# Epsilon as a column, balancing sums in PSUM, a lag of two blocks: eight small edits to a TensorE-bound kernel of attention and mixture of experts

## The chip, the cores and the metric

One core of a Trainium2 chip. The metric is device time in microseconds (us), the median of several runs; less is better. The engines are TensorE (PE in the profile, PEld its weight loads), VectorE (DVE), ScalarE (ACT), GpSimd (POOL) and SyncE (SP), whose queue issues the DMAs.

## The reference

Banded attention followed by a mixture of experts whose gate matrix is balanced by alternating row and column sums.

```python
# attention: q, k, v are (4, 8, 768, 64); n_global = 8, n_local = 96
scores = scale * q @ k.T + bias(|i - j|, head)       # kept where j < n_global or 0 <= i-j < n_local
a = np.exp(scores - max); a = a / (a.sum(-1) + 1e-09)
x = (a @ v) laid out as (3072, 512)
# experts: w_gate (512, 8), w1 (8, 512, 1024), w2 (8, 1024, 512)
P = np.exp(x @ w_gate - max)
for _ in range(8):
    P /= P.sum(1, keepdims=True) + 1e-09
    P /= P.sum(0, keepdims=True) + 1e-09
    P *= N / E
out = sum over e of P[:, e:e+1] * (np.maximum(x @ w1[e], 0) @ w2[e])
```

## The kernel before

All arithmetic is float32 precise: every operand is split into a high and a low part, and each product is three matmuls (high x low, low x high, high x high). The 3072 tokens are 24 tiles of 128, in three batches of 8 tiles (`BT`); the hidden columns are 31 groups (`NG`) of 256, the first 256 of expert 0 being done beside the attention. Within a batch, layer 1 of a group is a fast matrix product in seven products instead of eight (`FIRST`: p1 to p7, in banks x, y, z, w). The operands t1 to t4 that it needs are sums of blocks of x, made by `right_sums` on POOL or, for the last half batch, by `part_sum` on VectorE.

There are three stages in time.

1. *Attention*, to about 270 us. 32 units (4 batches, two halves, 4 pairs of heads) of three groups each. `softmax` (masked maximum on VectorE, line 342) and `exponentials` (ScalarE, line 356, which accumulates the row sums `sm`), then `inverses`: epsilon added (367), reciprocal (368), copied out to a tile (370) that `invert` turns on TensorE. Work of expert 0 (`filler`: h_ps, fhop, y_ps), the gate, and the block sums (lines 749 to 754) run between; `LEADS` says at which point of the last unit parts of the block sums of the last half batch are issued.
2. *The last batch, plainly*, about 270 to 930 us. For each group `layer1_fast`, then for each of 8 tiles a second layer (`layer2`, into y_ps), which is multiplied by the gate weight and added to `acc` (line 1235; for expert 0, line 1231, unweighted, and line 1234 multiplies by the weight of expert 0 once). Layer 1 of a group is interleaved with the second layer of the group before by `together(one, two, each, lead)`: one step of each in turn; with a `lead` of n, the second begins n steps later and what is left of it is handed back. The balancing (`sinkhorn`, 8 iterations of eight small VectorE operations and one matmul) runs through the first groups in steps, and its result `pm` is first needed by the second layer of the first group of expert 1, which runs beside layer 1 of the fifth group. Meanwhile ScalarE and POOL prepare the weights of later groups (`make_group`, lines 635, 636, 653).
3. *The other two batches, fast*, from about 930 us. Both layers use the seven products. `Fast.ended` makes the operands of the second layer (VectorE line 936, ScalarE 924, POOL 925 and 930). The second layer's seven products (m_ps, two PSUM buffers of two banks) are added up over 30 groups in SBUF tiles `ms` (line 1391; 1389 for the first group). After the 30th group `COMBINE` adds the seven sums together on POOL (line 1393). The 31st group is plain again: its y blocks are weighted and added to `acc`, and `back` turns the combined blocks on TensorE (c_ps) and adds them to `acc` (1411); then the tile goes out by DMA (1210). y_ps and c_ps share the two buffers of m_ps, except in the last batch, where y_ps uses the four banks of layer 1. `acc` is reloaded from DRAM with the part done in stage 1, and multiplied by the gate weight of expert 0 (line 1371), in group 2 of each batch.

The order on TensorE is that of the program (line 100 and 103 are the helper that keeps it). On the other engines a planner sets it: the framework simulates the program with its own costs and places each instruction when its inputs are ready. `issue_after` holds instructions behind a named one. PSUM tiles wait for the release of the buffer that they reuse.

The order of the products of the last combining group and of the tiles, which decide what must be ready first:

```python
LAST = tuple(SECOND[n] for n in (0, 3, 4, 2, 1, 6, 5))   # p1, p7, p6, p5, p3, p4, p2
ORDER = [n for i in (1, 0) for n in range(i, BT, 2)]     # 1, 3, 5, 7, 0, 2, 4, 6
BLOCKS = (("p2", "p4"), ("p3", "p5"))                    # turned for even and for odd tiles
```

Of the kernel before, what the change touches and what calls it, by code (L numbers as in the profile page):

```python
# [8 lines left out]
F32 = mybir.dt.float32  # L9
# [8 lines left out]
P = 128  # L18
# [25 lines left out]
LAST = tuple(SECOND[n] for n in (0, 3, 4, 2, 1, 6, 5))  # L44
COMBINE = {"p1": (("p6", "p1"),), "p6": (("p5", "p6"),), "p5": (("p3", "p5"), ("p5", "p7")),
           "p4": (("p4", "p6"), ("p4", "p7")), "p2": (("p2", "p1"),)}
# [59 lines left out]
class Banded:  # L106
# [4 lines left out]
    RAW = 4 * UT * P  # L111
    LEADS = (6 * CHUNK, 8 * CHUNK)

# [209 lines left out]
    def softmax(self, t, s_list):  # L323
# [37 lines left out]

    def inverses(self):

        nc, D = self.nc, self.D
        for n in self.summed:
            sm = self.sums[n]
            nc.vector.tensor_scalar(out=sm, in0=sm, scalar1=EPS, scalar2=None, op0=ALU.add)
            nc.vector.reciprocal(out=sm, in_=sm)
# [226 lines left out]
class Moe:  # L595
# [168 lines left out]

    def relu_split(self, src, t):
        nc = self.nc
        nc.scalar.activation(out=t[:, 0], in_=src, func=AF.Relu)
        self.low = nc.vector.scalar_tensor_tensor(out=t[:, 1], in0=src, scalar=0.0, in1=t[:, 0], op0=ALU.max,
                                                  op1=ALU.subtract)
# [96 lines left out]
    def sinkhorn(self, ps, tag):  # L866
# [16 lines left out]
        for _ in range(SINKHORN_ITERS):  # L883
            rsum = small.tile([P, TT], F32, name="rsum")
            nc.vector.tensor_reduce(out=rsum, in_=pm, op=ALU.add, axis=AX.X)
# [7 lines left out]
            nc.vector.tensor_reduce(out=csum, in_=c_ps.rearrange("p t e -> p e t"), op=ALU.add, axis=AX.X)  # L893
            nc.vector.tensor_scalar(out=csum, in0=csum, scalar1=EPS, scalar2=float(E) / N, op0=ALU.add, op1=ALU.mult)
# [55 lines left out]
def pipeline(tc, attention, ident, moe, acc):  # L950
# [11 lines left out]
    with ExitStack() as top:  # L962
# [126 lines left out]
        first, second = slice(0, 1), slice(1, KH)  # L1089
        stages = list(zip(attention.LEADS, ((("t1", slice(0, KH)),), (("t3", first), ("t2", first), ("t4", first)))))  # L1090
        tail = [(("t3", second),), (("t2", second), ("t4", second))]
# [119 lines left out]

        def plain_ops():
            hs = {}

            def ended(name, bank):
                hs[name] = hop.tile([P, 2, BU], F32R, name="hop")
                moe.relu_split(bank, hs[name])
            return hs, ended
# [3 lines left out]
        def second_plain(b, g, w, hs, new_ps, last, scaled, between=None):  # L1222

            e = groups[g][0]
            first_scaled = scaled is False and e != 0 and groups[g - 1][0] == 0
            for k, n in enumerate(ORDER):
                y_ps = new_ps(k)
                moe.layer2(n, w, hs, y_ps)
# [3 lines left out]
                else:  # L1232
                    if first_scaled:
                        nc.scalar.mul(a, a, moe.pm[:, tt, 0:1])
                    nc.vector.scalar_tensor_tensor(out=a, in0=y_ps, scalar=moe.pm[:, tt, e:e + 1], in1=a,  # L1235
                                                   op0=ALU.mult, op1=ALU.add)
# [32 lines left out]
        for g in range(NG):  # L1269
# [6 lines left out]
            def each(n):  # L1276
# [8 lines left out]
            prev = second_plain(b, g, w2, hs, lambda k: yps.tile([P, DM], F32, name="y_ps", tag="y"),  # L1285
                                g == NG - 1, False)
        for _ in sinkhorn:
            pass
# [38 lines left out]
        moe.in_order = False  # L1327
        mp = None
        for q, b in enumerate(order):
            x_ops, x_next = x_next, {}  # L1330
            ms = {}
            for g in range(NG):
# [7 lines left out]
                else:  # L1340
                    hs, ended = plain_ops()

# [19 lines left out]
                two = pend.pop(0)  # L1362
                rest = together(moe.layer1_fast(x_ops, w, mps, ltmp, ended), two, each, 0 if g < PLAIN else 2)
                if q == 0 and g == 0:
                    pss.close()
                    mp = top.enter_context(tc.tile_pool(name="mp", bufs=2, space=PSUM, reuse_waits="tile"))
                if g == 2:
                    for n in range(2):
                        nc.sync.dma_start(out=acc[:, n * HB:(n + 1) * HB], in_=y_spill[2 * b + n])
                    for n in range(BT):  # L1370
                        nc.scalar.mul(acc[:, n], acc[:, n], moe.pm[:, b * BT + n, 0:1])
                for load in loads:
# [3 lines left out]
                if g < PLAIN:  # L1376
                    def second_fast(hs=hs, w2=w2, g=g, ms=ms, seq=seq):
                        for p, a, o in seq:
# [11 lines left out]
                            else:  # L1390
                                nc.vector.tensor_tensor(out=ms[p], in0=bank, in1=ms[p], op=ALU.add)  # L1391
                            for to, by in COMBINE.get(p, ()) if g == PLAIN - 1 else ():
                                nc.gpsimd.tensor_tensor(out=ms[to], in0=ms[to], in1=ms[by], op=ALU.add)
                            yield
                    pend.append(second_fast())
                else:
                    last = q + 1 == len(order)

                    def new_ps(k, last=last):
                        if last:  # L1400
                            return mps.tile([P, BU], F32, name="y_ps", tag="h")
                        return mp.tile([P, 2, BU], F32, name="y_ps", tag="m")[:, 0]

                    def back(k, n, ms=ms):
# [85 lines left out]
```

## Time and profile before

| | us |
|---|---|
| median of 3 runs (lowest, highest) | 2115.78 (2114.74, 2116.29) |
| the profiled execution | 2115.21 |
| its span | 2113.4 |
| TensorE busy | 2089.2 |
| POOL busy | 1501.5 |
| VectorE busy | 1491.9 |
| ScalarE busy | 741.3 |

The granted clock of TensorE is 0.999 over the span. "Busy" of TensorE counts a matmul from its start to its modelled end, so that consecutive matmuls overlap; waits are read from the lists of who waited for whom and from the timeline, where the figure in brackets is the idle time of the engine before that instruction and the instruction that ended it. In a timeline row the columns are start, duration, engine, line, operation, output<-inputs, sizes, count. In a row for one line of the code the three numbers are the least, median and greatest duration in ns.

### The profile page before, as it was taken

The numbers are of one execution on the slowest core, as the hardware profiler recorded it, in microseconds if no ns is written. First come the engines' busy times: TensorE is split into PE (matmuls) and PEld (weight loads), VectorE is DVE, ScalarE is ACT, GpSimd is POOL, SyncE is SP. The second block draws the span as 40 slices with busy tenths as digits, with TensorE's granted clock in tenths as the row PEclk, the third lists the DMA queues.
The fourth block names the chain that finished last, engine by engine and source line by source line (L and its number), as shares of the span: only waits on it lengthen the run. The fifth ranks groups of instructions, "written<-read, shape, count | busy, mean of one in ns | idle before, by whom it ended". The sixth has DMA issues, their size and how long they took to land.

```text
span 2113.4 us, 31047 instructions
## 1 busy us (share of the span) xinstructions
PE 2089.2 (99%) x10437; PEld 1725.9 (82%) x10438; DVE 1491.9 (71%) x2292; ACT 741.3 (35%) x1538; POOL 1501.5 (71%) x1345
## 2 busy tenths in 40 slices
PE   9999999999999999999999999999999999999998
PEld 6888777888888888888888888888788888888886
DVE  8677688555565555557777777777677777777776
ACT  7888644333333323242222222222232222222221
POOL 4688787777777777357777777777677777777775
PEclk9999999999999999999999999999999999999999
DMA  6587676657566575697777777777977777677772
GB/s 144 127 224 200 188 270 233 251 209 268 214 234 239 209 261 209 257 368 204 203 194 203 205 195 202 204 202 201 363 212 196 202 204 204 193 203 204 194 194 77
DMA packets 294296, 452.40 MB, mean 214 GB/s; under 512 B 113584, under 2 KB 152688, under 8 KB 283760
## 3 DMA queue, kind: packets, MB, share of 16 engines
q1 hardware_dynamic: 294128, 450.31, 68.5%
q8 instruction: 87, 1.43, 0.3%
q14 instruction: 81, 0.66, 0.1%
HBM read 310.92 MB, written 139.30 MB: 213 GB/s over the span
## 4 chain that ended last, share of the span: by engine, by line
PE 91%; DVE 4%; ACT 3%; DMA 1%; issue 1%; POOL 0%; SPq 0%; ACTq 0%; DVEq 0%
PE m_ps L100 27%; PE y_ps L100 16%; PE bank_w L100 11%; PE bank_z L100 11%; PE bank_x L100 11%; PE bank_y L100 6%; PE o_ps L100 1%; PE s_ps L100 1%; PE t_ps L103 1%; PE h_ps L100 1%; DVE p_sb L342 1%; PE y_ps L829 1%; PE y_ps L830 1%; PE tp L103 1%; PE y_ps L828 0%
## 5 line engine op out<-in xcount | busy, mean ns | idle before, releaser
L100 PE MATMUL m_ps<-hop,w2r 128*128 128x512 f32 x2520 | 639.5, 389 | 2.0 <-DVE m L1391 1.4
L1391 DVE TENSOR_TENSOR m<-m_ps,m 128x1024 f32<-128x1024 f32 x406 | 495.3, 1220 | 194.6 <-PE m_ps L100 191.4
L100 PEld LDWEIGHTS m_ps<-hop,w2r 128*128 128x128 f32 x2520 | 472.8, 188 | 101.0 <-DVE m L1391 1.8
L925 POOL TENSOR_TENSOR hop<-h,hop 128x512 fp32r<-128x512 f32 x180 | 233.2, 1295 | 303.9 <-ACT hop L924 303.9
L100 PE MATMUL y_ps<-w2ops,hop 128*128 128x512 f32 x1344 | 336.9, 389 | 1.3 <-DVE acc L1235 1.3
L925 POOL TENSOR_TENSOR hop<-hsum,hop 128x512 fp32r<-128x512 f32 x240 | 305.2, 1293 | 1.1 <-ACT hop L924 0.9
L924 ACT CAST hop<-hsum 128x512 fp32r<-128x512 f32 x240 | 149.5, 623 | 425.8 <-POOL hsum L930 418.8
L100 PEld LDWEIGHTS y_ps<-w2ops,hop 128*128 128x128 f32 x1344 | 252.2, 188 | 53.8 <-DVE acc L1235 1.5
L1235 DVE SCALAR_TENSOR_TENSOR acc<-y_ps,pm,acc 128x512 f32<-128x512 f32 x240 | 179.8, 750 | 143.9 <-PE y_ps L100 142.1
L924 ACT CAST hop<-h 128x512 fp32r<-128x512 f32 x180 | 111.8, 621 | 379.2 <-DVE h L936 368.2
L100 PE MATMUL bank_w<-xr,w1r 128*128 128x512 f32 x744 | 189.0, 389 | 0.0
L100 PE MATMUL bank_z<-xr,w1r 128*128 128x512 f32 x744 | 189.0, 389 | 0.0
L100 PE MATMUL bank_x<-xr,w1r 128*128 128x512 f32 x744 | 188.9, 389 | 0.0
L930 POOL TENSOR_TENSOR hsum<-h,h 128x512 f32<-128x512 f32 x120 | 153.1, 1297 | 40.8 <-DVE h L936 40.7
L100 PEld LDWEIGHTS bank_x<-xr,w1r 128*128 128x128 f32 x744 | 139.5, 188 | 28.9
L100 PEld LDWEIGHTS bank_w<-xr,w1r 128*128 128x128 f32 x744 | 139.5, 188 | 28.9
L100 PEld LDWEIGHTS bank_z<-xr,w1r 128*128 128x128 f32 x744 | 139.5, 188 | 28.9
L930 POOL TENSOR_TENSOR hsum<-h,hsum 128x512 f32<-128x512 f32 x120 | 155.5, 1296 | 0.0
L653 POOL TENSOR_TENSOR wsum<-w1f 128x256 f32<-128x256 f32 x62 | 44.7, 742 | 94.9 <-DMA w1f<-in_moe_w_dram 94.9
L356 ACT ACTIVATE p_sb<-p_sb,mx 128x256 f32<-128x256 f32 (+1 forms) x192 | 93.5, 496 | 7.4 <-DVE mx L342 6.7
L100 PE MATMUL bank_y<-xr,w1r 128*128 128x512 f32 x372 | 94.4, 389 | 0.0
L802 DVE TENSOR_TENSOR t<-bank_y,t 128x512 f32<-128x512 f32 x93 | 64.3, 691 | 40.3 <-PE bank_y L100 38.2
(261 smaller groups left out, 3347.2 us busy)
## 6 DMA issues: line engine op xcount, KB each, us to landing
w1r<-w1s SPq DMA_DIRECT2D x434, 256.0 KB, 3.0
w2r<-w2s SPq DMA_DIRECT2D x420, 256.0 KB, 3.0
w1s<-w1ops SPq DMA_DIRECT2D x31, 1792.0 KB, 6.8
w2s<-s2ops SPq DMA_DIRECT2D x30, 1024.0 KB, 8.6
w2s<-w2ops SPq DMA_DIRECT2D x30, 768.0 KB, 7.7
w1f<-in_moe_w_dram SPq DMA_DIRECT2D x32, 512.0 KB, 7.9
w2f<-in_moe_w_dram SPq DMA_DIRECT2D x32, 512.0 KB, 8.5
xs_t<-piece SPq DMA_DIRECT2D x16, 512.0 KB, 4.3
```

The costliest lines, as they stand in the source:

```text
L100: return self.tc.keep_in_program_order(self.engine.matmul(*args, **kw))
L103: return self.tc.keep_in_program_order(self.engine.transpose(*args, **kw))
L342: nc.vector.tensor_tensor_reduce(out=pv, in0=s_list[u], in1=bias, scale=-(D ** -0.5), scalar=3.0e38, op0=ALU.add, op1=ALU.min, accum_out=m ...
L356: nc.scalar.activation(out=pv, in_=pv, func=AF.Exp, bias=mx[:, u:u + 1], scale=-1.0, accum_out=sm[:, i, j:j + 1])
L653: self.nc.gpsimd.tensor_tensor(out=s[:, n], in0=x, in1=y, op=op)
L802: tt(out=t, in0=bank["y"], in1=t, op=ALU.add)
L829: self.pe.matmul(y_ps, lhsT=hl, rhs=wf, start=False, stop=False, skip_group_check=True)
L924: self.nc.scalar.copy(out=t[:, 0], in_=full)
L925: self.nc.gpsimd.tensor_tensor(out=t[:, 1], in0=full, in1=t[:, 0], op=ALU.subtract)
L930: self.nc.gpsimd.tensor_tensor(out=t, in0=self.full[x], in1=self.full[y], op=ALU.subtract)
L1235: nc.vector.scalar_tensor_tensor(out=a, in0=y_ps, scalar=moe.pm[:, tt, e:e + 1], in1=a, op0=ALU.mult, op1=ALU.add)
L1391: nc.vector.tensor_tensor(out=ms[p], in0=bank, in1=ms[p], op=ALU.add)
```

## The change

Eight edits.

1. Epsilon is written once into a second column beside each row sum (tile `eps`, four slots); the sums accumulate into the first column, and a reduction over the two columns takes the place of the addition.
2. In the balancing, the row sums lie in a PSUM tile of their own and the column sums in a last row of the PSUM tile that the matmul wrote.
3. The block sum t1 of the last half batch is made in two halves, at points 12 and 18 of the last unit; it was made whole at 18.
4. In the fifth group of stage 2, the second layer begins two products later (`lead`), and what is left of it goes ahead of the next group's.
5. In the 31st group of stage 3, the low part of b21 is taken (`relu_low`) after the most recent m add; it followed the high part at once.
6. y and c blocks take four buffers of one bank each, opened when the m buffers are closed; the m buffers are opened again in each batch. Each `back` runs two tiles behind its y, and the last ones one and none behind.
7. `acc` is multiplied by the weight of expert 0 in group 4, behind an m add; it was in group 2.
8. p3 and p5 are combined after p3's last add (it was after p5's), in two halves of the tokens.

```diff
-COMBINE = {..., "p5": (("p3", "p5"), ("p5", "p7")), ...}
+COMBINE = {..., "p3": (("p3", "p5"), ("p5", "p7")), ...}
-    LEADS = (6 * CHUNK, 8 * CHUNK)
+    LEADS = (4 * CHUNK, 6 * CHUNK, 8 * CHUNK)
...
+        self.eps = self.wrk.tile([P, 4, UT, 2, 2], F32, name="eps", bufs=1)
+        tc.nc.gpsimd.memset(self.eps, EPS)
-            self.sums[n] = self.wrk.tile([P, UT, 2], F32, name="sm", bufs=4)
+            self.sums[n] = self.eps[:, n % self.eps.shape[1]]
-                                     accum_out=sm[:, i, j:j + 1])
+                                     accum_out=sm[:, i, j, 0:1])
-            sm = self.sums[n]
-            nc.vector.tensor_scalar(out=sm, in0=sm, scalar1=EPS, scalar2=None, op0=ALU.add)
+            sm = self.wrk.tile([P, UT, 2], F32, name="sm", bufs=2)
+            nc.vector.tensor_reduce(out=sm, in_=self.sums[n], op=ALU.add, axis=AX.X)
...
     def relu_split(self, src, t):
+        self.relu_high(src, t)
+        self.relu_low(src, t)
...
-            rsum = small.tile([P, TT], F32, name="rsum")
+            rsum = ps.tile([P, TT], F32, name="rsum", tag=tag)
-            c_ps = ps.tile([P, TT, E], F32, name="c_ps", tag=tag)
-            self.pe.matmul(c_ps, lhsT=ones, rhs=pm, start=True, stop=True)
-            csum = small.tile([P, E], F32, name="csum")
+            c_ps = ps.tile([P, TT + 1, E], F32, name="c_ps", tag=tag)
+            self.pe.matmul(c_ps[:, 0:TT], lhsT=ones, rhs=pm, start=True, stop=True)
+            csum = c_ps[:, TT]
...
-        stages = ... ((("t1", slice(0, KH)),), (("t3", first), ("t2", first), ("t4", first)))
+        stages = ... ((("t1", first),), (("t1", second),), (("t3", first), ("t2", first), ("t4", first)))
...
# second_plain: the returned blocks lag
-                if between is not None:
-                    between(k, n)
-                if last:
-                    out_tile(b, n)
+                lagging.append(n)
+                while len(lagging) > (2 if between is not None and k < BT - 2 else 1 if between is not None and k < BT - 1 else 0):
+                    ended = lagging.pop(0)
+                    if between is not None:
+                        between(ended)
+                    if last:
+                        out_tile(b, ended)
...
# stage 2
-            together(moe.layer1_fast(x_ops, w[0], mps, ltmp, ended), prev, each)
+            lead = 2 if g > 1 and groups[g - 1][0] > groups[g - 2][0] == 0 else 0
+            rest = together(moe.layer1_fast(x_ops, w[0], mps, ltmp, ended), prev, each, lead)
+            if lead:
+                prev = after(rest, prev)
...
# stage 3
+                if g >= PLAIN:
+                    with tc.issue_after(moe.added.ins):
+                        moe.relu_low(*late[0])
-                if q == 0 and g == 0:
-                    mp = top.enter_context(tc.tile_pool(name="mp", bufs=2, space=PSUM, reuse_waits="tile"))
+                if g == 0:
+                    sums_ps.close()
+                    mp = sums_ps.enter_context(tc.tile_pool(name="mp", bufs=2, space=PSUM, reuse_waits="tile"))
-                    for n in range(BT):
-                        nc.scalar.mul(acc[:, n], acc[:, n], moe.pm[:, b * BT + n, 0:1])
+                if g == 4:
+                    with tc.issue_after(moe.added.ins):
+                        for n in range(BT):
+                            nc.scalar.mul(acc[:, n], acc[:, n], moe.pm[:, b * BT + n, 0:1])
-                                nc.vector.tensor_tensor(out=ms[p], in0=bank, in1=ms[p], op=ALU.add)
-                            for to, by in COMBINE.get(p, ()) if g == PLAIN - 1 else ():
-                                nc.gpsimd.tensor_tensor(out=ms[to], in0=ms[to], in1=ms[by], op=ALU.add)
+                                moe.added = nc.vector.tensor_tensor(out=ms[p], in0=bank, in1=ms[p], op=ALU.add)
+                            for h in (slice(0, BU // 2), slice(BU // 2, BU)) if p == "p3" else (slice(0, BU),):
+                                for to, by in COMBINE.get(p, ()) if g == PLAIN - 1 else ():
+                                    nc.gpsimd.tensor_tensor(out=ms[to][:, :, h], in0=ms[to][:, :, h], in1=ms[by][:, :, h], op=ALU.add)
-                    def new_ps(k, last=last):
-                        if last:
-                            return mps.tile([P, BU], F32, name="y_ps", tag="h")
-                        return mp.tile([P, 2, BU], F32, name="y_ps", tag="m")[:, 0]
+                    tps = []
+                    def new_ps(last=last, tps=tps):
+                        if not tps:
+                            sums_ps.close()
+                            tps.append(sums_ps.enter_context(tc.tile_pool(name="tps", bufs=4, space=PSUM, reuse_waits="tile")))
+                        return (mps if last else tps[0]).tile([P, BU], F32, name="y_ps", tag="h")
...
-                        t_ps = mp.tile([P, 2, BU], F32, name="c_ps", tag="m")[:, 0]
+                        t_ps = tps[0].tile([P, BU], F32, name="c_ps", tag="h")
```

More of the change, by code (lines that the diff above doesn't have):

```diff
@@ L44 @@
 LAST = tuple(SECOND[n] for n in (0, 3, 4, 2, 1, 6, 5))
-COMBINE = {"p1": (("p6", "p1"),), "p6": (("p5", "p6"),), "p5": (("p3", "p5"), ("p5", "p7")),
+COMBINE = {"p1": (("p6", "p1"),), "p6": (("p5", "p6"),), "p3": (("p3", "p5"), ("p5", "p7")),
            "p4": (("p4", "p6"), ("p4", "p7")), "p2": (("p2", "p1"),)}
@@ L765, in relu_split, with relu_high, relu_low @@
     def relu_split(self, src, t):
+        self.relu_high(src, t)
+        self.relu_low(src, t)
+    def relu_high(self, src, t):
+        self.nc.scalar.activation(out=t[:, 0], in_=src, func=AF.Relu)
+    def relu_low(self, src, t):
         nc = self.nc
-        nc.scalar.activation(out=t[:, 0], in_=src, func=AF.Relu)
         self.low = nc.vector.scalar_tensor_tensor(out=t[:, 1], in0=src, scalar=0.0, in1=t[:, 0], op0=ALU.max,
@@ L889, in sinkhorn @@
             yield
-            c_ps = ps.tile([P, TT, E], F32, name="c_ps", tag=tag)
-            self.pe.matmul(c_ps, lhsT=ones, rhs=pm, start=True, stop=True)
-            csum = small.tile([P, E], F32, name="csum")
-            nc.vector.tensor_reduce(out=csum, in_=c_ps.rearrange("p t e -> p e t"), op=ALU.add, axis=AX.X)
+            c_ps = ps.tile([P, TT + 1, E], F32, name="c_ps", tag=tag)
+            self.pe.matmul(c_ps[:, 0:TT], lhsT=ones, rhs=pm, start=True, stop=True)
+            csum = c_ps[:, TT]
+            nc.vector.tensor_reduce(out=csum, in_=c_ps[:, 0:TT].rearrange("p t e -> p e t"), op=ALU.add, axis=AX.X)
             nc.vector.tensor_scalar(out=csum, in0=csum, scalar1=EPS, scalar2=float(E) / N, op0=ALU.add, op1=ALU.mult)
@@ L1089, in pipeline @@
         first, second = slice(0, 1), slice(1, KH)
-        stages = list(zip(attention.LEADS, ((("t1", slice(0, KH)),), (("t3", first), ("t2", first), ("t4", first)))))
+        stages = list(zip(attention.LEADS, ((("t1", first),), (("t1", second),), (("t3", first), ("t2", first), ("t4", first)))))
         tail = [(("t3", second),), (("t2", second), ("t4", second))]
@@ L1210, in out_tile, with plain_ops @@
             nc.sync.dma_start(out=moe.out[tt * P:(tt + 1) * P, :], in_=acc[:, n])
-        def plain_ops():
+        def plain_ops(late=None):
             hs = {}
@@ L1216, in ended @@
                 hs[name] = hop.tile([P, 2, BU], F32R, name="hop")
-                moe.relu_split(bank, hs[name])
+                if late is None or name != "b21":
+                    moe.relu_split(bank, hs[name])
+                else:
+                    moe.relu_high(bank, hs[name])
+                    late.append((bank, hs[name]))
             return hs, ended
@@ L1224, in second_plain @@
             e = groups[g][0]
+            lagging = []
             first_scaled = scaled is False and e != 0 and groups[g - 1][0] == 0
             for k, n in enumerate(ORDER):
-                y_ps = new_ps(k)
+                y_ps = new_ps()
                 moe.layer2(n, w, hs, y_ps)
@@ L1282, in each @@
                     steps(n)
-            together(moe.layer1_fast(x_ops, w[0], mps, ltmp, ended), prev, each)
+            lead = 2 if g > 1 and groups[g - 1][0] > groups[g - 2][0] == 0 else 0
+            rest = together(moe.layer1_fast(x_ops, w[0], mps, ltmp, ended), prev, each, lead)
             w2 = w[1]
-            prev = second_plain(b, g, w2, hs, lambda k: yps.tile([P, DM], F32, name="y_ps", tag="y"),
+            prev = second_plain(b, g, w2, hs, lambda: yps.tile([P, DM], F32, name="y_ps", tag="y"),
                                 g == NG - 1, False)
+            if lead:
+                prev = after(rest, prev)
         for _ in sinkhorn:
@@ L1327, in pipeline @@
         moe.in_order = False
-        mp = None
+        sums_ps, mp = top.enter_context(ExitStack()), None
         for q, b in enumerate(order):
@@ L1340, in pipeline @@
                 else:
-                    hs, ended = plain_ops()
+                    late = []
+                    hs, ended = plain_ops(late)
                 nxt, loads = (g + 1) % NG, []
@@ L1397, in pipeline, with back @@
                     last = q + 1 == len(order)
-                    def new_ps(k, last=last):
-                        if last:
-                            return mps.tile([P, BU], F32, name="y_ps", tag="h")
-                        return mp.tile([P, 2, BU], F32, name="y_ps", tag="m")[:, 0]
-                    def back(k, n, ms=ms):
+                    tps = []
[4 more added lines that the diff above has]
+                        return (mps if last else tps[0]).tile([P, BU], F32, name="y_ps", tag="h")
+                    def back(n, ms=ms, tps=tps):
                         i, j = n % 2, n // 2
-                        t_ps = mp.tile([P, 2, BU], F32, name="c_ps", tag="m")[:, 0]
+                        t_ps = tps[0].tile([P, BU], F32, name="c_ps", tag="h")
                         for d, p in enumerate(BLOCKS[i]):
```

## The prediction

> **What bounds the kernel now.** I read the page first (engine totals), then busy time by stage, then who waits for whom on TensorE, and last the timeline around every wait.
>
> ```profile
> span 2113.4 us, 31047 instructions
> PE 2089.2 (99%) x10437; PEld 1725.9 (82%) x10438; DVE 1491.9 (71%) x2292; ACT 741.3 (35%) x1538; POOL 1501.5 (71%) x1345
> L100 PE MATMUL m_ps<-hop,w2r 128*128 128x512 f32 x2520 | 639.5, 389 | 2.0 <-DVE m L1391 1.4
> 100.00:150.00 50.00, 49.56 (x492) 42.55 (x489) 39.23 (x139) 45.34 (x146) 41.30 (x53) 1.00 0.77 208
> 500.00:600.00 100.00, 100.00 (x442) 82.80 (x442) 58.99 (x84) 32.47 (x53) 71.64 (x69) 1.00 0.60 227
> ```
>
> Columns of the stage rows: window, length, busy time (and instructions) of PE, weight loads, VectorE, ScalarE and POOL, granted clock, DMA share, GB/s. TensorE is the bound. At 500 to 600 it starts 442 matmuls in 100 us without a gap, one per 0.226 us; one matmul lasts 0.389 us and covers the next. So a matmul that waits costs the idle time shown plus 0.389 - 0.226 = 0.16 us. The change removes no TensorE work. All it can win is waits. Those that lie at its places:
>
> ```profile
> PE y_ps L100 <- DVE acc L1235: 2.5, 4, 1.3
> PE y_ps L829 <- DVE hop L768: 1.5, 1, 1.5
> PE m_ps L100 <- DVE m L1391: 1.4, 1, 1.4
> PE y_ps L100 <- DVE fhop L768: 1.2, 1, 1.2
> PE t_ps L103 <- DVE mx L342: 0.8, 1, 0.8
> PE m_ps L100 <- ACT m L1389: 0.5, 1, 0.5
> PE r_ps L103 <- ACT inv L370: 0.3, 1, 0.3
> ```
>
> Ten waits (columns: total, times, longest), 8.2 us idle, 9.8 us with 0.16 us each. I looked up each in the timeline and ask which edit reaches it.
>
> **Edit 1, epsilon as a column.** It removes 32 additions (L367) and adds 32 small reductions over two columns, plus one memset.
>
> ```profile
> L367 DVE TENSOR_SCALAR sm<-sm x32: 161/568/1303, 14.4 to 236.0; 128x6 f32<-128x6 f32 x32
> L885 DVE TENSOR_REDUCE rsum<-pm x8: 338/353/353, 281.4 to 349.2; 128x24 f32<-128x192 f32 x8
> 157.66 1.27 POOL L740 TENSOR_TENSOR xsum<-xsum,xres 128x512 f32<-128x512 f32 x1
> 157.84 1.12 DVE L367 TENSOR_SCALAR sm<-sm 128x6 f32<-128x6 f32 x1
> 159.44 0.63 PE L103 MATMUL t_ps<-ident,p_sb 128*128 128x128 f32 x4 [0.81 <-DVE mx L342]
> ```
>
> The addition of six numbers takes 0.16 to 1.30 us; the one at 157.84 ends at 158.96, just after POOL's instruction (158.93). It stands behind POOL. A reduction keeps 0.338 to 0.353 us eight times, in the stage where an addition of 24 numbers reaches 1.97 us (L886, below). The new reduction costs between 0.16 (the quickest addition of six) and 0.35 us (a reduction of 192 numbers); it reads 12, so I take 0.18. At the median VectorE gets back 32 x (0.57 - 0.18) = 12.5 us, nearly all of it off the path. On the path I find one place: the addition at 157.84 holds up the masked maxima (L342) behind it, and TensorE waits 0.81 us for them and then 0.33 us for the inverse made from that sum: 1.14 + 2 x 0.16 = 1.46. I take **1.4 us** (0 to 2). The memset is one POOL instruction of 48 columns before any exponential; no wait of TensorE on POOL is among the rows, so I cost it at nothing, and at most at the 1.27 us that 512 columns take.
>
> **Edit 2, balancing sums in PSUM.**
>
> ```profile
> L886 DVE TENSOR_SCALAR rsum<-rsum x8: 178/766/1970, 281.8 to 350.1; 128x24 f32<-128x24 f32 x8
> L896 DVE TENSOR_TENSOR pm<-pm,csum x8: 357/1280/2253, 291.3 to 355.4; 128x192 f32<-128x192 f32 x8
> L809 DVE TENSOR_TENSOR bank_y<-bank_w,u x93: 689/700/700, 276.4 to 2079.9; 128x512 f32<-128x512 f32 x93
> L881 DVE TENSOR_SCALAR gm<-ngm_ps x1: 149/149/149, 277.0 to 277.0; 128x1 f32<-128x1 f32 x1
> 281.36 2.39 POOL L636 TENSOR_TENSOR w1ops<-wsum,w1ops 128x1024 fp32r<-128x1024 f32 x1
> 281.82 1.97 DVE L886 TENSOR_SCALAR rsum<-rsum 128x24 f32<-128x24 f32 x1
> 284.44 0.50 PE L829 MATMUL y_ps<-w2ops,hop 128*128 128x512 f32 x1 [1.54 <-DVE hop L768]
> ```
>
> With both inputs in SBUF, L896 stretches up to sixfold; L809, one input in PSUM, keeps 0.69 to 0.70 us 93 times. So the operations with PSUM operands should stop stretching. At 281.82 the addition lasts 1.97 us and ends with POOL's (283.75); the residual behind it (L768) releases TensorE at 284.44. At 0.18 us the residual starts 1.8 us sooner, and the wait of 1.54 + 0.16 = 1.70 goes; what is late next is the matmul in front, by less than 0.1. I take **1.6 us** (0 to 1.7). The sums share one PSUM buffer with the column sums, but each step of the balancing needs the one before it already: no new wait.
>
> [...]
>
> **Edit 3, staged sums in halves.**
>
> ```profile
> 244.06 1.66 DVE L752 TENSOR_TENSOR piece<-piece 128x512 f32<-128x512 f32 x1
> 245.64 0.68 DVE L768 SCALAR_TENSOR_TENSOR fhop<-h_ps,fhop 128x512 fp32r<-128x512 f32 x1
> 252.77 1.40 DVE L752 TENSOR_TENSOR piece<-piece 128x256 f32<-128x256 f32 x1
> ```
>
> t1 is made in two halves, one of them a chunk earlier. The full-width sums delay fhop, and TensorE waits 1.20 us (1.36 with the overlap). Half a sum is not half the time: a half-width one also took 1.40 us behind POOL. The second half stays where the whole was, so I take **0.5 us** of 1.36 (ends: 1.4 won, 1.0 lost, if the earlier half now holds up other VectorE work).
>
> **Edit 4, a two-product lead in the fifth group.**
>
> ```profile
> 346.04 0.40 PE L100 MATMUL bank_x<-xl,w1ops 128*128 128x512 f32 x1
> 355.38 0.36 DVE L896 TENSOR_TENSOR pm<-pm,csum 128x192 f32<-128x192 f32 x1
> 357.68 1.66 PE L100 MATMUL y_ps<-w2ops,hop 128*128 128x512 f32 x6 [1.28 <-DVE acc L1235]
> ```
>
> These y blocks are the first that need the gate weights. Three banks fill before the weights are final (355.74), and the fourth block waits 1.28. With the lead, six products and three blocks of 6 x 0.226 = 1.36 us come ahead of the fourth block (now four and three): it starts 12.2 us after the group's start, at 358.3 and not at 355.9, while the last balancing matmul, issued at a fixed step, has two blocks fewer ahead of it. The wait goes: **1.4 us** (1.28 + 0.16). Three blocks pass into the next group. The weight splits on ScalarE and POOL that reuse the buffer of these blocks, and the loads on SP behind them, come some 8 us later once; they run one group (15 x 1.36 = 20 us) ahead of their use, which hides it. Without that cover the cost would be the excess over 20 us. I take none.
>
> **Edits 5 and 6, four banks with a lag of two, scaling moved to group 4.**
>
> ```profile
> 1510.28 1.66 PE L100 MATMUL y_ps<-w2r,hop 128*128 128x512 f32 x6 [0.41 <-DVE acc L1235]
> 1526.10 2.56 ACT L1371 ACTIVATE acc<-acc,pm 128x512 f32<-128x512 f32 x4 [2.17 <-DMA acc<-ys]
> 1530.22 1.15 PE L100 MATMUL m_ps<-hop,w2r 128*128 128x512 f32 x4 [0.55 <-ACT m L1389]
> ```
>
> At the change of batch y and c share two buffers, so y waits for the add of the y before it, three times 0.41 + 0.16 = 1.71. With four banks each y or c waits for the fourth tile before it, two pairs (over 3 us) back: gone. ScalarE stands in the scaling (waiting for the DMA) and delivers the first m copies late: 0.55 + 0.16 = 0.71. Moved two groups on and behind an m add, the eight scalings (2.56 / 4 = 0.64 us each, 5.1 us) find the data landed; queued behind them are casts for POOL, on an engine that is busy a third of the time at 500 to 600 (32.47 of 100). Together **2.4 us**. The output DMAs go two blocks later; the reload behind them on SP then has until group 4.
>
> **Edits 7 and 8, the end: late residual, p3 combined by halves.**
>
> ```profile
> 2086.26 0.69 DVE L815 TENSOR_TENSOR bank_w<-bank_w,t 128x512 f32<-128x512 f32 x1
> 2088.23 2.35 DVE L1391 TENSOR_TENSOR m<-m_ps,m 128x1024 f32<-128x1024 f32 x2
> 2089.50 1.67 PE L100 MATMUL m_ps<-hop,w2r 128*128 128x512 f32 x6 [1.41 <-DVE m L1391]
> 2092.40 0.60 PE L103 MATMUL c_ps<-ident,m 128*128 128x128 f32 x4
> 2092.75 1.63 PE L100 MATMUL y_ps<-w2r,hop 128*128 128x512 f32 x6
> L1393 POOL TENSOR_TENSOR m<-m x14: 2382/2402/2415, 1479.7 to 2095.9; 128x1024 f32<-128x1024 f32 x14
> 2106.26 0.69 DVE L1411 TENSOR_TENSOR acc<-c_ps,acc 128x512 f32<-128x512 f32 x1
> ```
>
> The last m product waits for a bank until VectorE's add of 2088.23, which stands behind the b21 residual. With the residual after it, and p3's add no longer behind POOL, the add runs 2086.95 to 2088.2 and the product starts 1.25 us sooner. It gives back a little: after the last y two c adds follow instead of one (0.69 more), but that y ends a c (2092.40 to 2092.75, with the switch 0.45) earlier: +0.25. POOL starts combining at 2088.2 with four halves (1.27 each, the 512-column sum above) and three whole sums (2.40), 12.3 us, and ends near 2100.6. The first block that needs p2 and p4 comes after the m product, seven y (1.36 each) and four c (0.35, and 0.1 at the switch): 2088.2 + 10.9 + 1.8 = 2100.9. That margin of 0.3 us is thin. **1.0 us** net (0 to 1.4).
>
> **Sum.** 1.4 + 0.5 + 1.6 + 1.4 + 2.4 + 1.0 = 8.3 us. The profiled execution took 2115.21, 0.57 below the median of the runs (2115.78). 2115.21 - 8.3 = 2106.9; on the median 2107.5.
>
> **The rivals.**
> - *The first 360 us give nothing* (0.17). The order of instructions there is a planner's, and changed operations reorder VectorE and ScalarE; waits of 0.5 to 1.5 us come back elsewhere. For it: ScalarE is busy 45.34 of 50 us there. Against: the waits are isolated. Left are 2.4 + 1.0 = 3.4: 2112.4. The variant that PSUM operands still wait for POOL loses 1.6 and perhaps the lead's 1.4: 2110.5.
> - *New waits at the new places* (0.15). The scalings as a burst of 5 us hold the casts that feed POOL once per batch, and POOL's combining misses its 0.3 us: 2 x 1.2 (an estimate: a quarter of the burst uncovered) + 0.6 = 3 us, 2110.5.
> - *More than the sum* (0.08). VectorE's 13 us shorten many small waits of the attention stage: 12 us, 2103.8.
> - *Slower* (0.08). The running sums of four units become one tile. If ScalarE's next exponentials must wait for the reduction there, it is on an engine at 0.91 busy. It decides from (8.3 + 4.2) / 32 = 0.39 us per unit on; at 0.5 us each, 2123.5. Against: L367 holds the same order today.
>
> **How the numbers follow.** A measurement here tells about 0.2% (4.2 us) from no change: faster is below 2111.5. The sum as worked out has 0.52, with 2104.5 to 2110.5 by its bounds. Faster: 0.52 + 0.15 + 0.08 = 0.75; within: 0.17; slower: 0.08. The range 2104.0 to 2112.8 takes in the first two rivals and leaves out the slow case and most of the fast one.
>
> **What would show it.** Right: no wait of y on L1235 at the change of batch or near 357; L886 and L896 at about 0.18 and 0.36 us; no wait of y at L829; the last m product 0.1 to 0.2 us behind its predecessor. Wrong: new waits on kk, qq or mx before 250 us, m or c waiting for POOL at the end, or hop waiting for ScalarE in group 4.

## The result, and the profile after

The changed kernel takes 2139.22 us (median; 2137.51 to 2141.44) against 2115.78 before: a ratio of 1.0114, with a 95% interval of 1.0099 to 1.0129. It is slower, by 23.4 us, and outside the predicted range.

The page of the changed kernel, its first lines and two of its costliest groups (columns: busy us, mean ns of one):

```profile
span 2139.0 us, 31111 instructions
PE 2119.7 (99%) x10437; PEld 1728.2 (81%) x10438; DVE 1468.7 (69%) x2296; ACT 741.8 (35%) x1539; POOL 1505.0 (70%) x1350
...
L100 PE MATMUL m_ps<-hop,w2r 128*128 128x512 f32 x2520 | 645.7, 391 | 0.0
L100 PE MATMUL bank_w<-xr,w1r 128*128 128x512 f32 x744 | 192.8, 394 | 0.0
```

The same group of layer 1 on the page of before:

```profile
L100 PE MATMUL bank_w<-xr,w1r 128*128 128x512 f32 x744 | 189.0, 389 | 0.0
```

The same 10437 matmuls, 30.5 us more busy time than before (2089.2), and less idle time (2139.0 - 2119.7 = 19.3 us against 24.2). The mean of one matmul, up to its modelled end, is longer: in these groups layer 2 went from 389 to 391 ns, layer 1 from 389 to 394. Busy time of overlapping matmuls says little on the pace, so the next view is the number of matmuls in a stretch without waits. By stage, changed kernel (window, length, busy time and count of TensorE, of weight loads, VectorE, ScalarE, POOL; granted clock, DMA share, GB/s):

```profile
500.00:600.00 100.00, 100.00 (x436) 81.52 (x435) 58.70 (x84) 33.09 (x54) 70.73 (x68) 1.00 0.62 232
1200.00:1300.00 100.00, 100.00 (x435) 81.39 (x434) 75.51 (x84) 24.95 (x42) 72.68 (x59) 1.00 0.71 201
```

and the second stretch in the kernel before:

```profile
1200.00:1300.00 100.00, 100.00 (x443) 82.80 (x442) 77.22 (x86) 24.62 (x42) 72.23 (x58) 1.00 0.72 199
```

TensorE is full in both, at the same granted clock (1.00), with about the same DMA traffic (201 and 199 GB/s); it starts 435 matmuls in 100 us in place of 443. Measured from start to start over the full-width matmuls (512 columns) that follow one another without a wait, from 60 us on, the mean is 226.9 ns before (8170 pairs, 1853.7 us in all) and 230.5 ns after (8175 pairs, 1884.3 us): 30.6 us lost. That is more than the whole loss, and it is spread over everything from 270 us to the end. Within a run of one layer, from 960 us on, layer-1 matmuls start 232.5 ns apart (before 226.7), those of layer 2 229.7 (226.7). In the attention stage, up to 270 us, the pace is the same in both (230.2 and 230.3 ns).

What the edits aimed at did mostly go. Who waited for whom on TensorE, changed kernel, the first lines of the whole list:

```profile
PE s_ps L100 <- DVE kk L276: 2.0, 2, 1.4
PE y_ps L100 <- ACT fhop L772: 1.8, 1, 1.8
PE y_ps L100 <- DVE acc L1248: 1.8, 1, 1.8
PE gt_ps L103 <- ACT acc L864: 1.6, 2, 1.2
PE w_ps L100 <- DVE acc L1475: 1.5, 1, 1.5
```

No y waits at L837 for hop, no m for VectorE or ScalarE, no t for the maxima. But one wait of y for acc (L1248) is still there, and the waits for ScalarE at L772 and L864 are new or longer.

What can slow every matmul of layer 1 at the same clock? None of the edits touches a matmul of layer 1. But edit 2 takes `rsum` (96 bytes per partition) and `csum` (32) out of SBUF, and they were allocated from the left-hand side, ahead of the tiles of x: every tile allocated there after them moves down by 128 bytes. In the compiled kernels x of layer 1 begins at byte 46976 of each partition before and at 46848 after: 384 and 256 modulo 512. The weights it is multiplied with are allocated from the other end and did not move (384 modulo 512 in both). The theory, then: **a matmul is slowed when the operand that it streams and the weights loaded beside it lie at different places modulo some power of two.** The rivals: the four banks, the sums in PSUM or the new order of instructions slow TensorE; or it is the place of x by itself.

### The profile page after: what moved, and what is told of

It is laid out like the page before. It is cut to its first block, busy times and chain, and to the rows that moved or that the text cites. A ratio compares the mean times of both kernels' runs of the same rounds, so it can differ in the third digit from the quotient of the medians.

```text
span 2139.0 us, 31111 instructions
## 1 busy us (share of the span) xinstructions
PE 2119.7 (99%) x10437; PEld 1728.2 (81%) x10438; DVE 1468.7 (69%) x2296; ACT 741.8 (35%) x1539; POOL 1505.0 (70%) x1350
## 4 chain that ended last, share of the span: by engine, by line
PE 97%; ACT 1%; DVE 1%; issue 0%; DMA 0%; POOL 0%; DVEq 0%; ACTq 0%
PE m_ps L100 27%; PE y_ps L100 17%; PE bank_w L100 12%; PE bank_x L100 12%; PE bank_z L100 12%; PE bank_y L100 6%; PE o_ps L100 2%; PE t_ps L103 2%; PE s_ps L100 2%; PE h_ps L100 1%; PE tp L103 1%; PE y_ps L837 1%; PE y_ps L838 1%; PE y_ps L836 1%; ACT p_sb L358 0%; PE r_ps L103 0%
## 5 line engine op out<-in xcount | busy, mean ns | idle before, releaser
L1248 DVE SCALAR_TENSOR_TENSOR acc<-y_ps,pm,acc 128x512 f32<-128x512 f32 x240 | 179.8, 750 | 147.6 <-PE y_ps L100 146.0
```

## The experiments

**1. The 128 bytes put back.** Changed kernel, with an unused width on a small tile of the same pool:

```
-        gmax = small.tile([1, 1], F32, name="gmax")
+        gmax = small.tile([P, 33], F32, name="gmax")[0:1, 0:1]
```

> The changed kernel with one small constant tile widened by 128 bytes per partition, so that the SBUF tiles allocated after it (the split input, x of layer 1, its pieces) lie at the addresses modulo 512 that they had before the change; nothing else differs. Placement theory: the full matmuls start 226.7 ns apart again in place of 230.5, some 30.6 us come back, and the time is 2107 to 2110 us. Rival, that another part of the change (the four banks, the sums in PSUM, the order of instructions) slows the matmuls: the pace stays 230.5 and the time stays at 2139.

2111.59 us; ratio to the kernel before 0.998 (0.9971 to 0.9989).

```profile
1200.00:1300.00 100.00, 100.00 (x443) 82.81 (x442) 77.19 (x86) 24.76 (x42) 72.45 (x58) 1.00 0.72 199
```

443 matmuls again, a pace of 226.9 ns: 27.6 us come back from a tile that nothing reads. (The time is 1.6 us above the expected 2107 to 2110; that part is taken up below.) All edits of the change are in this kernel, so none of them slows TensorE otherwise.

**2. The kernel before, moved.** None of the edits; the same small tile 384 bytes wider, so that x lies at 256 modulo 512 (`tile([P, 97], ...)[0:1, 0:1]`).

> The kernel before with the same small tile widened by 384 bytes, so that the left-hand tiles lie 256 modulo 512 as in the changed kernel; none of the change's edits. Placement theory: the pace falls from 226.7 to about 230.5 ns and the time rises by some 30 us to 2142 to 2148. Rival: nothing changes, 2116.

2144.43 us, ratio 1.0135 (1.0119 to 1.015), pace 230.5.

```profile
1200.00:1300.00 100.00, 100.00 (x435) 81.40 (x434) 75.23 (x84) 25.21 (x43) 72.66 (x59) 1.00 0.72 201
```

The same 435 as in the changed kernel. With experiment 1 this settles the cause: place, in both directions, with the edits and without them.

**3. Both sides moved.** Changed kernel, the tile at the far end of the right-hand side 128 bytes wider:

```
-    edge = ctx.enter_context(tc.tile_pool(name="edge", bufs=1, side="right")).tile([P, 24], F32, name="edge")
+    edge = ctx.enter_context(tc.tile_pool(name="edge", bufs=1, side="right")).tile([P, 56], F32, name="edge")
```

> The changed kernel with the 96-byte tile at the far end of the right-hand side widened by 128 bytes, so that the right-hand tiles (weights, products) move down by 128 and lie 256 modulo 512 like the left-hand ones. If only the distance between the matmuls' two sides counts: fast again, 2107 to 2110. If the address of each tile counts (384 modulo 512 good, 256 bad): 2139 or slower, to 2145. If placement does not matter: 2139.

2107.86 us, ratio 0.9966 (0.9954 to 0.9978), pace 226.9.

```profile
1200.00:1300.00 100.00, 100.00 (x443) 82.84 (x442) 76.42 (x85) 25.68 (x44) 74.02 (x59) 1.00 0.71 200
```

Both operands now lie at 256 modulo 512 and the loss is gone: the distance counts, not the place. This version is faster than the kernel before and than the changed one.

**4. Edit 2 undone** (`rsum` and `csum` as tiles of SBUF again, which also restores the places).

> The changed kernel with edit 2 undone: the balancing sums in SBUF again, which also puts the 128 bytes back ahead of the other tiles. Placement theory: pace 226.7, about 2109 to 2111 (the 1.6 us of the wait that edit 2 removed come back). Theory that the sums in PSUM slow TensorE by themselves: the same figure, so this run is read with the first one. Theory that the four banks or the order of instructions slow it: 2139.

2110.51 us, ratio 0.9975 (0.9965 to 0.9984), pace 226.9. As expected of the placement; its 1.1 us less than experiment 1 lies within the spread of the two (2108.73 to 2112.82 and 2109.45 to 2113.05), so the worth of edit 2 is not to be read from this time. Its trace does show again the wait that edit 2 was to remove: y for hop at L837, 0.9 us (1.5 before; none in experiments 1 and 3).

**5. Edit 3 undone**, on the kernel of experiment 3 (`LEADS` with two entries, t1 in one piece).

> The changed kernel with the right-hand tiles moved down by 128 bytes (as in the run that measured 2107.9) and edit 3 undone: the sum t1 in one piece at its old due time. Theory from the traces: in the changed kernel the ScalarE copy of the first half of t1 waits 4.5 us at 227 for VectorE's sums and holds up the exponentials behind it, so gate's transposes wait 1.2 us and the last fhop 1.8 us; undone, 232 to 246 gets 2.4 us shorter: 2105.0 to 2106.5. Rival, that these waits come from the earlier arrival of the other work (edit 1) and not from edit 3: no gain, 2107.5 to 2108.5.

2107.41 us, ratio 0.9963 (0.9949 to 0.9976): not told apart from experiment 3, and above the 2105.0 to 2106.5 that were expected. The two waits of TensorE that the expectation names did go (1.2 and 1.8 us), but the wait of y for VectorE's fhop (L776) grew from 0.6 to 2.0 us, and others came. TensorE's waits from 225 to 285 us without edit 3:

```profile
PE y_ps L100 <- DVE fhop L776: 2.0, 1, 2.0
PE s_ps L100 <- ACT acc L389: 0.5, 1, 0.5
PE bank_x L763 <- POOL w1ops L638: 0.3, 1, 0.3
```

and 0.4 more at 344. From 3.6 us of waits (1.8, 1.2 and 0.6) 2.7 are left; the last m matmul starts 1.0 us earlier (2082.62, against 2083.62), and what follows gives back more than half of that (spans of 2104.1 and 2104.5). The expected 2.4 us were the loss at one place, not at the end.

**6. The kernel before with both sides moved** (384 bytes on the left, 128 on the right).

> The kernel before with both sides moved, left up by 384 bytes and right down by 128, so that all of them lie 256 modulo 512. The distance theory expects the pace of before, 226.7 ns, and 2116. It also asks why the changed kernel with the right side moved (2107.9) beat the one with the left side moved back (2111.6), though their matmuls after 270 us are equally fast: if the place of the attention tiles modulo 512 is worth these 3.7 us, this kernel shows it too, 2112 to 2113; if it belongs to the change, 2116.

2116.01 us, ratio 0.9998 (0.9989 to 1.0007). From 1200 to 1300 us TensorE starts 443 matmuls, as before: the distance theory holds once more. It does not say why experiment 3 beat experiment 1; that is taken up below.

**7, 8, 10 and 11. Other distances.** The kernel before with the left-hand side 32, 256, 64 and 224 bytes up; a single run each.

> The kernel before with the left-hand tiles moved up by 32 bytes: x of layer 1 lies 416 modulo 512, its weights 384. If every difference in the address modulo 512 costs the same: pace 230.5, 2145. If the cost grows with the distance: 226.7 to 228, 2116 to 2126. If only the address modulo 128 or less counts, the distance of 128 of the runs before could not have cost anything; that is out already.

> The kernel before with the left-hand tiles moved up by 256 bytes: x of layer 1 lies 128 modulo 512, its weights 384. If the cost goes by the address modulo 256: no loss, pace 226.7, 2116. If modulo 512: a loss, pace 230.5 or more, 2145 or more; if it grows with the distance, above the 2144 measured at 128.

> The kernel before with the left-hand tiles 64 bytes up (64 apart from the weights modulo 256). Known by now: 0 and 256 apart cost nothing, 128 apart 28 us, 32 apart 42 us. If the loss falls as the distance grows from 32 to 128: between 2144 and 2158. If every distance that is no multiple of 64 has its own cost and 64 is a boundary: near 2116 to 2144.

> The kernel before with the left-hand tiles 224 bytes up, which is 32 below a multiple of 256. If only the size of the distance counts: as 32 above, 2158. If its sign counts (x of layer 1 begins late or early in its line of 256): another time, 2130 to 2150.

| distance of x to its weights, modulo 256 | time, us | pace, ns | matmuls from 1200 to 1300 us |
|---|---|---|---|
| 0 (before) | 2115.8 | 226.9 | 443 |
| 0 (256 up) | 2117.1 | 226.9 | 443 |
| 128 (experiment 2) | 2144.4 | 230.5 | 435 |
| 64 | 2154.2 | 231.1 | 434 |
| 32 | 2158.3 | 232.1 | 432 |
| 224, that is 32 below | 2156.7 | 232.0 | 433 |

256 costs nothing (2117.1 lies within the runs of the kernel before beside it, 2114.8 to 2118.3), so at the distances tried the cost goes by the address modulo 256. It does not grow with the distance: of those tried it is greatest at 32, on either side alike (2158.3 and 2156.7 are not told apart by single runs), and least, but not nothing, at 128. The time at 32 is above all that had been expected of it; 64, 224 and 256 each came as one of the cases expected. The row of the dearest, 32 bytes:

```profile
1200.00:1300.00 100.00, 100.00 (x432) 80.84 (x432) 74.31 (x83) 23.69 (x40) 69.49 (x55) 1.00 0.72 199
```

**9. The changed kernel, left side 384 bytes up**: 256 from the weights.

> The changed kernel with the left-hand tiles moved up by 384 bytes, so that x of layer 1 lies 128 modulo 512 and its weights 384: 256 apart. If the cost goes by the address modulo 256, the pace is 226.7 ns and the time 2107 to 2112 (between the two other placements without a loss, which measured 2107.9 and 2111.6); if the address modulo 512 counted, 2139 or more.

2110.99 us, ratio 0.9978 (0.9968 to 0.9988), pace 226.9: that 256 bytes cost nothing holds in the changed kernel too.

**12. Only the layer-1 weights of the third stage moved.** Changed kernel:

```
+        top.enter_context(tc.tile_pool(name="apart", bufs=1, side="right")).tile([P, 32], F32, name="apart")
         w1r = top.enter_context(tc.tile_pool(name="w1r", bufs=8, side="right", reuse_waits="tile"))
```

> The changed kernel with 128 unused bytes ahead of the layer-1 weights of the third stage alone (after 900 us), so that there x of layer 1 and its own weights both lie 256 modulo 512, while hop and the layer-2 weights stay at 384; the stage before is left as it is. If a matmul is slowed by the distance between the x that it streams and the layer-1 weights loaded beside it: after 960 the pace is 226.7 ns again, or up to 228.1 since the two changes between the layers in each twelve matmuls still meet at a distance of 128; 346 to 900 stays at 230.3; the time is 2119 to 2126. If the distance of x to hop or to the layer-2 weights counts (the layer-2 matmuls are slowed too, though their own operands agree): no gain, 2139 or more.

(The tile behind these weights, `h32`, moves with them.) 2125.52 us, ratio 1.0049 (1.0032 to 1.0066), inside the expected range; the pace is 0.2 ns above the expected bound.

```profile
500.00:600.00 100.00, 100.00 (x436) 81.51 (x435) 58.17 (x83) 32.22 (x53) 70.47 (x68) 1.00 0.59 221
1200.00:1300.00 100.00, 100.00 (x440) 82.52 (x439) 75.35 (x84) 24.89 (x42) 73.60 (x59) 1.00 0.70 202
```

436 in the second stage as in the changed kernel, 440 in the third. The mean there is 228.3 ns, and the records show where the rest sits: of the six starts in a layer's run the middle four are 226 or 227 ns apart (medians from 1000 to 1400 us), while the last of a run takes 233 and the first of the next 231. Those are the changes between the layers, where the streamed operand and the weights loaded beside it still lie 128 apart. Ten ns at each of two changes in twelve matmuls are 1.7 ns each, the difference of 228.3 and 226.7. The change from layer 2 to layer 1 tells the pair apart: there hop is streamed, at 384, while layer-1 weights are loaded. In the changed kernel these lie at 384 too, and the change takes 227 ns (median) though x and its own weights disagree; in experiment 12 they lie at 256, and it takes 233. So the reading that fits is that the distance between the operand that is being streamed and the next weights, loaded beside it, counts, whichever tensors they are. It does not say when the loss shows: in the changed kernel the starts within a run of layer 2, whose own operands agree, are 232, 233 and 231 ns apart before they are back at 227, so on this reading the loss made in a run of layer 1 comes out up to three starts late (one in experiment 12, five in experiment 7). Why is not shown.

## Why the prediction was wrong

**The step that failed** is in its first part: "The change removes no TensorE work. All it can win is waits." From that it followed, unsaid, that all it can lose is waits as well. Edit 2 was costed on VectorE and in PSUM alone; that SBUF loses 128 bytes ahead of every tile of layer 1 was in the diff, and no step asked what moves when a tile goes. In the sum the pace of the matmuls, 0.226 us each, stood as fixed; the change of place made it 230.5 ns in place of 226.9. Its worth was 1884.3 - 1853.7 = 30.6 us of pace. No rival had it: the slower one was a wait of ScalarE for the eps tile in the attention stage, and there the changed kernel is not behind (its last s_ps starts at 229.92 us, that of before at 232.56).

With the places restored the time is 2107.9 us in experiment 3 and 2111.6 and 2111.0 in 1 and 9, against 2107.5 predicted. That experiment 3 lands within 0.4 us of it is luck: edits 3 and 4 missed by 2.9 and 1.7 us, and 4.3 us that no step had make up for them. Term by term, as the shift of the same matmul between the trace of before and that of experiment 3 (the numbers are those of the prediction, whose edits 5 and 6 are 6 and 7 in the list of the change, and whose 7 and 8 are 5 and 8 there):

| step of the prediction | predicted | measured |
|---|---|---|
| edit 1, at 159 us | -1.4 | -1.3 |
| edit 3, 232 to 246 us | -0.5 | +2.4 |
| edit 2, at 284 us | -1.6 | -1.8 |
| edit 4, at 357 us | -1.4 | +0.3 |
| edits 5 and 6, 928 to 1530 us | -2.4 | -2.7 |
| edits 7 and 8, at 2089 us | -1.0 | -1.5 |
| no step: attention -1.5 in all, bank_x at 280 us -0.8, after the last matmul -1.6, the rest -0.4 | 0 | -4.3 |
| span, 2113.4 to 2104.5 | -8.3 | -8.9 |

*Edits 1, 2 and the prediction's 5 to 8 came near their figures,* but two of the gains not in the way that was worked out. The rows of experiment 3 that answer for them:

```profile
L369 DVE TENSOR_REDUCE sm<-eps x32: 153/161/167, 14.8 to 236.4; 128x6 f32<-128x12 f32 x32
L894 DVE TENSOR_SCALAR rsum<-rsum x8: 181/190/192, 280.4 to 347.5; 128x24 f32<-128x24 f32 x8
L904 DVE TENSOR_TENSOR pm<-pm,c_ps x8: 340/354/354, 288.1 to 355.0; 128x192 f32<-128x192 f32 x8
2081.69 2.32 PE L100 MATMUL m_ps<-hop,w2r 128*128 128x512 f32 x8
2097.51 1.04 PE L103 MATMUL c_ps<-ident,m 128*128 128x128 f32 x8
```

The reduction over 12 numbers takes 0.153 to 0.167 us all 32 times, the addition with its operands in PSUM 0.190 where it took up to 1.97, L904 at most 0.354 where L896 took up to 2.25. (For 24 numbers the quickest addition is 0.181 us with both ends in PSUM, and it was 0.178 with both in SBUF: by itself the place in PSUM costs 0.003 us here.) The last eight m matmuls run without an idle time, and the last c starts at 2097.51; in the kernel before the last y and c start at

```profile
2103.73 1.64 PE L100 MATMUL y_ps<-w2r,hop 128*128 128x512 f32 x6
2105.21 0.60 PE L103 MATMUL c_ps<-ident,m 128*128 128x128 f32 x4
```

From 1480 us on no wait of TensorE is left.

Edit 1 was to remove two waits, 0.81 us for the maxima and 0.33 for the inverse. The second is still there (0.34 at 158.23); that the sum of 1.4 fits the measured 1.3 is luck, since the first alone moved the next transpositions by 1.2 us and not by 0.81 + 0.16. And the scalings of `acc` did not go to group 4:

```profile
1524.28 2.56 ACT L1398 ACTIVATE acc<-acc,pm 128x512 f32<-128x512 f32 x4
1534.32 1.22 DVE L1418 TENSOR_TENSOR m<-m_ps,m 128x1024 f32<-128x1024 f32 x1 [2.65 <-PE m_ps L100]
```

The four at 1524.28 and the four after them (from 1528.16) still stand among the first m copies of the batch, ahead of its first m add at 1534.32: `issue_after` did not hold these ScalarE instructions behind an add on VectorE. What went is their wait of 2.17 us for the load of `acc`. SyncE issues the two loads at 1515.69 and 1519.86 us, where the kernel before issued them at 1518.23 and 1526.76; which edit brought the second forward was not tried.

*Edit 3 failed at its lower end, and beyond it:* "1.0 lost, if the earlier half now holds up other VectorE work". That condition came true at the first half; at the second half ScalarE was held up too, which no step had. Experiment 3, the timeline of VectorE, ScalarE and TensorE at that place:

```profile
228.21 0.98 PE L100 MATMUL s_ps<-kk,qq 64*128 64x256 f32 x12 [0.50 <-ACT acc L389]
230.30 1.40 DVE L754 TENSOR_TENSOR piece<-piece 128x256 f32<-128x256 f32 x1
231.63 0.41 DVE L344 CUSTOM_DVE_ANT_0 p_sb<-s_ps,acc 128x256 f32<-128x256 f32 x1
231.97 0.07 DVE L344 DVE_READ_ACCUMULATOR2_ANT mx<- 128x1 f32 x1
...
231.78 0.41 ACT L755 CAST xh<-piece 128x256 fp32r<-128x256 f32 x1 [3.14 <-POOL xl L743]
232.09 0.51 ACT L358 ACTIVATE p_sb<-p_sb,mx 128x256 f32<-128x256 f32 x1
...
235.34 0.56 ACT L864 COPY acc<-g_ps 16x512 f32<-16x512 f32 x1
...
243.88 0.40 ACT L755 CAST xh<-piece 128x256 fp32r<-128x256 f32 x1 [3.02 <-DVE piece L754]
244.19 0.59 ACT L772 ACTIVATE fhop<-h_ps 128x512 fp32r<-128x512 f32 x1
...
235.95 0.42 PE L103 MATMUL gt_ps<-ident,acc 16*128 16x16 f32 x4 [1.18 <-ACT acc L864]
244.83 0.50 PE L100 MATMUL y_ps<-w2l,fhop 128*128 128x512 f32 x1 [1.77 <-ACT fhop L772]
```

and experiment 5, without edit 3, the first maximum:

```profile
228.85 0.42 DVE L344 CUSTOM_DVE_ANT_0 p_sb<-s_ps,acc 128x256 f32<-128x256 f32 x1 [0.80 <-PE s_ps L100]
```

Each half is three sums on VectorE and then a cast on ScalarE (L755). At the first half the sums stand ahead of the masked maxima (L344): the first maximum starts 3.42 us after s_ps, right behind the sum of 230.30, and without edit 3 it starts 0.90 us after s_ps (228.85 and 227.95). The exponentials wait for their maxima, the gate's copy (L864) stands behind them, and TensorE waits 1.18 us for the gate. The cast ahead of the exponentials costs next to nothing, though ScalarE stands idle 3.14 us before it: the first exponential starts at 232.09, and the maximum that it needs is read out until 232.04. (The view names POOL as the releaser of that cast; VectorE's sum ends at 231.70, and the cast starts 0.08 later.) At the second half it is the cast that costs: ScalarE stands idle 3.02 us for the sum, with fhop behind the cast, where the one whole cast of before came after fhop (245.80 and 244.03); TensorE waits 1.77. The prediction asked what the halves do on the engine that computes them and not what they do on the engine that ends them.

Not all of the 2.4 us is the edit's. Without it, in experiment 5, the same stretch still shifts by +0.8, since y waits 1.96 us for the low part of fhop on VectorE (1.20 before). At the last m matmul, undoing edit 3 is worth 1.0 us.

*Edit 4 failed in "two blocks fewer ahead of it".* What counts is the distance from the last balancing matmul to the first y block that needs its result. Experiment 3:

```profile
353.20 0.49 PE L899 MATMUL c_ps<-pm,ones 128*128 128x192 f32 x2
353.39 0.99 PE L100 MATMUL y_ps<-w2ops,hop 128*128 128x512 f32 x3
...
355.43 0.65 DVE L913 COPY pt_in<-pm 128x64 f32<-128x64 f32 x1
356.23 0.27 PE L916 MATMUL pt_ps<-ident,pt_in 128*64 128x128 f32 x1 [0.46 <-DVE pt_in L913]
357.51 0.96 PE L100 MATMUL y_ps<-w2ops,hop 128*128 128x512 f32 x3 [1.02 <-DVE acc L1248]
```

and the kernel before:

```profile
354.01 0.49 PE L891 MATMUL c_ps<-pm,ones 128*128 128x192 f32 x2
354.20 0.52 PE L100 MATMUL y_ps<-w2ops,hop 128*128 128x512 f32 x1
354.57 1.55 PE L100 MATMUL bank_z<-xh,w1ops 128*128 128x512 f32 x6
```

Between them lie three y matmuls and six of bank z where there were one and six. The lead moved the balancing along with the blocks: its last matmul starts 10.70 us after the first of the fifth group (353.20 and 342.50), where it was 7.97 before (354.01 and 346.04). (The prediction's 355.9 is also 0.3 late: seven times 1.36 us after 346.04 are 355.6.) The distance grew by two matmuls, 0.45 us. The wait fell from 1.28 to 1.02, and the transposition ahead of it waits 0.46 for a copy (L913) that takes 0.65 us in place of 0.22. Nothing is won.

*The -4.3 us that no step had* are not the change's for sure. Between two kernels that differ in unused bytes alone, experiment 3 and experiment 1, the start of the last s_ps differs by 2.5 us (229.71 and 232.19; before 232.56). Experiment 1, three of TensorE's waits from 160 to 240 us:

```profile
PE tp L103 <- DMA raw<-in_k_dram: 0.8, 1, 0.8
PE s_ps L100 <- DVE inv L488: 0.8, 2, 0.6
PE o_ps L100 <- DMA acc<-in_v_dram: 0.5, 1, 0.5
```

There a transposition behind edit 1's place waits for a load of k that experiment 3 finds landed in that stretch. So edit 1's gain stays in one of these traces and is mostly given back in the other. Each trace is one execution, and executions of one changed kernel differ by as much (2109.45 to 2113.05 in experiment 1, 2107.17 to 2111.38 in experiment 3), though the medians differ too. Why the load lands later is open: experiment 6 shows that in the kernel before the place of the attention tiles alone changes nothing, and nothing else was tried.

The prediction's first rival, "The first 360 us give nothing" (2112.4), is closer to most of the versions with the places restored. The same layer-1 matmul, at 500 us, is shifted against the kernel before by -3.0 us in experiment 3 and -4.0 in 5, but by -0.1 in 1, +2.4 in 4 and +3.0 in 9 (the traced executions of 3 and 5 are the shortest of theirs, those of 4 and 9 near the longest, 2112.55 and 2112.92). The medians of 1, 4 and 9, 2110.5 to 2111.6, lie nearer to it than to 2107.5. From there to the end all five win 4.6 to 5.9 us. The change with its places restored is therefore worth 4 to 8 us (experiments 1, 9 and 3; ratios of 0.998, 0.9978 and 0.9966), and not a single figure.

## What to carry to other kernels

A tile that leaves a pool, or changes its size, moves every tile behind it (here by 128 bytes); where TensorE is the bound, compare the addresses of the streamed operands and of the weights modulo 256 before and after an edit, and pad to keep them equal (here 226.9 ns from start to start when they were equal, 230.5 at 128 bytes). When a full engine is slower at the same granted clock and with no new waits, count instructions per stretch and look for what they share, not for what the edits meant to do. For work that is split or moved, look at the queue of every engine that it passes, the one that finishes it too: an early instruction, or one that cannot run yet, holds all that stands behind it (here the first maximum, 3.42 us after s_ps behind the early sums and 0.90 without them; and fhop, behind a cast for whose sum ScalarE stood idle 3.02 us). And look in the trace whether an instruction that was told to move did.

## What the runs showed of the hardware

- Matmuls of 128x512 (fp32r in the rows of their operands) with a weight load each start 226.9 ns apart, in the mean over this kernel, when the streamed operand and the weights lie at the same address modulo 256, 230.5 at a distance of 128, 231.1 at 64 and 232.1 at 32 bytes; in a kernel of 2116 us that is up to 42 us, at a granted clock of 0.999.
- The cost fits the pair of a streaming matmul and the load of the next weights: with 128 bytes between the layers alone (experiment 12), about 10 ns at each change of layer (starts 233 and 231 ns apart, the others 226 or 227), part of it one start later. What makes the pair slower, why the loss can show some starts late, and why 32 bytes (232.1 ns) are worse than 128 (230.5), stays open.
